# Loads unit by unit in the order of need, full-array kv and inter, and crossbar transposes from unit 10 on, in a linear-attention and bilinear-FFN kernel

## Chip, cores, metric

One core of one Trainium2 chip. The metric is device time in microseconds (us). "Span" is the time from the first to the last instruction in a profiled run; a run's time is about 2 us longer than its span. The diffs are shortened; words in them stand for longer code.

## The reference

Block-recurrent linear attention with a decay per head (4 batches, 8 heads, 768 positions, 64 dims), then a bilinear FFN on its output:

```python
for b in range(nb):                      # blocks of 64 positions
    intra = einsum('bhic,bhjc->bhij', qb, kb) * Dmask      # lam ** (i-j), lower triangle
    out_b = einsum('bhij,bhjd->bhid', intra, vb) + einsum('bhid,bhde->bhie', qb*lam_pow, kv)
    kv = lam**block * kv + einsum('bhsd,bhse->bhde', kb*rev_pow, vb)
x = out.transpose(0, 2, 1, 3).reshape(3072, 512)
y = ((x @ w_a) * (x @ w_b)) @ w_out      # w_a, w_b: 512 x 1536, w_out: 1536 x 512; all float32
```

## The kernel before

The kernel works in units of 128 positions of one batch, with all 8 heads; 24 units, 6 to a batch. It scales q and k by powers of lam, so that the decay needs only a triangle mask and a running state. Four units make a group of 512 tokens. While TensorE does one group's FFN, "hooks" between its matmuls insert the attention of the next group: `prep` (scale q and k, cast v), T (transpose q and k), K (the scores and their mask), O (output, inter from the state, and the state's update kv). Slots 0 to 11 are the hooks after each of the 12 chunks of a and b, slots 12 to 19 lie in the op matmuls, two per token tile. The schedule is written by hand: each engine has its instructions in one fixed order, and all DMAs are issued from one queue, SP's, in a fixed order too.

```python
def load_batch(b, n0=0, n1=NB):
    ...                                   # allocate qf, kf, vf of the whole batch, two buffers each
    for t, src in zip(batch_tiles[b], (qr, kr, vr)):
        if n0 == 0 and n1 == NB:          # whole batch: 1.5 MB per tensor
            nc.sync.dma_start(out=t[:].rearrange("p h nb d -> p (h nb) d"), in_=...)
        else:                             # tensor by tensor, unit by unit
            for nb in range(n0, n1):
                nc.sync.dma_start(out=t[:, :, nb, :], in_=src[b, :, :, nb, :])

def piece_T(u):                           # 8 transposes on TensorE, copied out by ScalarE
    for j, src in enumerate((d["qs"], d["ks"])):
        for hp in range(HP):
            nc.tensor.transpose(tps[:, j, hp, :], src[:, 2 * hp:2 * hp + 2, :], ident)
    nc.scalar.copy(qkT, tps)

def piece_O(u, xT, col):
    ...                                   # 8 matmuls vb x masked scores, then, in half arrays:
    for hp in range(HP):
        for i in range(2):
            p = slice(64 * i, 64 * i + 64)
            nc.tensor.matmul(o_ps[p, hp, :], lhsT=st[p, hp, :], rhs=qkT[p, 0, hp, :], ...)        # inter
    ...
            nc.tensor.matmul(kvd[p, hp, :], lhsT=ks[:, 2 * hp + i, :], rhs=vb[:, 2 * hp + i, :], ...)  # kv
    nc.vector.tensor_copy(st, kvd)

# order of loads: units 0-3, w_a and w_b chunk 0, w_a chunk 1; then
load_w("b", 1); load_w("a", 2); load_batch(0, UPG, NB)          # units 4 and 5
preps = {0: 0, 3: 1, 8: 2, 12: 3}
base, offs = [0, 4, 9, 14], [(1, 2, 4), (1, 2, 4), (1, 2, 3), (1, 2, 3)]   # slots of T, K, O
def hook(slot):
    if g == 0:
        ...
        if slot == 3: ...; load_w("o", 1)
        if slot == 4: ...; load_w("o", 2); load_batch(1)
    if slot in preps:
        u = nxt * UPG + preps[slot]
        prep(u)
        if u % NB == NB - 1 and u // NB + 2 < B:
            load_batch(u // NB + 2)
    ...
```

## Time and profile before

| | before |
|---|---|
| time, median of 3 | 306.51 us (304.59 to 306.56) |
| span, profiled run | 304.6 us, mean granted clock 0.938 |
| TensorE busy | 238.3 us, 78% |
| lead-in (to the first a_ps matmul) | 35.1 us |
| first group's FFN | 79.9 us |
| a later group of four | 38.4 us |

Busy shares mix stages with different limits. What matters is where TensorE waits: the lead-in, and a hole from 58 to 92 us in the first group. The prediction below shows those lines. In SP's timeline (start, duration, queue, source line, DMA), whole-batch loads have line L92.

### The profile page before, as it was taken

What the parts mean: (1) busy time and instruction counts of PE and PEld (TensorE: products, weight loads), DVE (VectorE), ACT (ScalarE), POOL (GpSimd) and SP (SyncE); (2) the same over time, 40 slices, a digit from 0 to 9 for tenths busy, and PEclk for the clock granted to TensorE, in tenths of its full rate; (3) what the DMA queues carried; (4) which work ended last, traced back from release to release, by engine and by line L of the source; (5) the groups of instructions that cost most, each with busy time, mean ns of one, the idle gap of its engine ahead of it and who ended that gap; (6) DMA issues with size and microseconds to landing.
All of it is one profiled execution on the core that took longest, in us unless ns stands there. A gap on an engine that the chain in (4) does not pass through costs nothing.

```text
span 304.6 us, 4308 instructions
## 1 busy us (share of the span) xinstructions
PE 238.3 (78%) x1760; PEld 116.0 (38%) x1760; DVE 102.6 (34%) x168; ACT 103.3 (34%) x156; POOL 53.5 (18%) x56
## 2 busy tenths in 40 slices
PE   0205899600007699999999999999999999999995
PEld 0104544200002254444444444454454444444442
DVE  2113695000002523464125542264512554213410
ACT  4027475200002134533344334434344343333321
POOL 1500332000019621212212121212211000000000
PEclk9999999955557799999999999999999999999999
DMA  7999969999997016930910001100011000110002
GB/s 146 218 337 387 219 221 290 218 218 277 217 218 138 37 69 157 220 75 22 253 72 0 2 0 74 67 3 0 2 69 69 3 0 2 69 71 0 0 34 103
DMA packets 41059, 34.87 MB, mean 114 GB/s; under 512 B 19536, under 2 KB 33360, under 8 KB 41040
## 3 DMA queue, kind: packets, MB, share of 16 engines
q1 hardware_dynamic: 41040, 34.61, 46.1%
q8 instruction: 13, 0.21, 0.3%
q14 instruction: 6, 0.05, 0.1%
HBM read 28.32 MB, written 6.29 MB: 114 GB/s over the span
## 4 chain that ended last, share of the span: by engine, by line
PE 66%; SPq 16%; DMA 8%; DVE 5%; issue 2%; ACT 2%; DVEq 0%; ACTq 0%
PE op L255 19%; PE a_ps L242 18%; PE b_ps L248 17%; SPq L92 9%; DMA vf<-in_v_dram 5%; SPq L96 4%; PE tps L182 3%; DVE m L199 3%; DMA wst<-in_moe_w_b_dram 3%; PE o_ps L210 2%; SPq L109 2%; PE kq L194 2%; PE o_ps L217 2%; PE kvd L227 1%; DVE ab L250 1%
## 5 line engine op out<-in xcount | busy, mean ns | idle before, releaser
L250 DVE TENSOR_TENSOR ab<-a_sb,b_ps 128x512 bf16<-128x512 bf16 x72 | 49.3, 687 | 86.0 <-PE b_ps L248 85.8
L242 PE MATMUL a_ps<-xT,wa_sb 128*128 128x512 bf16 x288 | 75.0, 383 | 0.4 <-ACT xT L219 0.4
L248 PE MATMUL b_ps<-xT,wb_sb 128*128 128x512 bf16 x288 | 74.8, 383 | 0.0
L255 PE MATMUL op<-wo_sb,ab 128*128 128x512 bf16 x288 | 68.3, 387 | 0.0
L245 ACT CAST a_sb<-a_ps 128x512 bf16<-128x512 f32 x72 | 42.2, 587 | 58.3 <-PE a_ps L242 58.3
L199 DVE TENSOR_TENSOR m<-kq,lotri 128x512 bf16<-128x512 f32 x48 | 30.8, 683 | 35.2 <-PE kq L194 35.1
L248 PEld LDWEIGHTS <-wb_sb 128*128 128x128 bf16 x288 | 28.4, 98 | 34.6 <-issue 1.1
L184 ACT COPY qkT<-tps 128x1024 bf16<-128x1024 bf16 x24 | 24.2, 1013 | 45.1 <-PE tps L182 45.1
L169 POOL TENSOR_TENSOR qs<-qf,lp_q 128x512 bf16<-128x512 f32 x20 | 20.8, 1041 | 102.1 <-PE tps L182 49.7
L255 PEld LDWEIGHTS <-ab 128*128 128x128 bf16 x288 | 26.7, 99 | 30.9 <-issue 2.3
L170 POOL TENSOR_TENSOR ks<-kf,lp_k 128x512 bf16<-128x512 f32 x24 | 26.3, 1098 | 65.9 <-PE kvd L227 39.3
L242 PEld LDWEIGHTS <-wa_sb 128*128 128x128 bf16 x288 | 26.1, 98 | 27.9 <-issue 1.0
L182 PE MATMUL tps<-ident,qs 128*128 128x128 bf16 x96 | 10.4, 238 | 32.6 <-POOL qs L169 26.2
L260 ACT COPY o_sb<-op 128x512 f32<-128x512 f32 x24 | 14.0, 585 | 46.8 <-PE op L255 46.8
L174 DVE CAST vb<-vf 128x512 bf16<-128x512 f32 x20 | 10.8, 540 | 42.7 <-DMA vf<-in_v_dram 42.7
L219 ACT CAST xT<-o_ps 128x512 bf16<-128x512 f32 x24 | 14.0, 585 | 30.1 <-PE o_ps L217 18.7
L182 PEld LDWEIGHTS <-qs 128*128 128x128 bf16 x96 | 7.7, 106 | 37.8 <-POOL qs L169 26.7
L194 PE MATMUL kq<-qkT 64*128 64x128 bf16 x192 | 10.3, 231 | 14.0 <-ACT qkT L184 14.0
L182 PE MATMUL tps<-ident,ks 128*128 128x128 bf16 x96 | 10.4, 238 | 10.8 <-POOL ks L170 10.7
L210 PE MATMUL o_ps<-m,vb 128*64 128x128 bf16 x192 | 11.6, 230 | 4.8 <-DVE m L199 4.2
L194 PEld LDWEIGHTS <-qkT 64*128 64x128 bf16 x192 | 5.8, 99 | 23.6 <-ACT qkT L184 16.8
L210 PEld LDWEIGHTS <-vb 128*64 128x64 bf16 x192 | 7.0, 112 | 14.7 <-issue 8.4
(26 smaller groups left out, 65.3 us busy)
## 6 DMA issues: line engine op xcount, KB each, us to landing
out_dram<-o_sb SPq DMA_DIRECT2D x24, 256.0 KB, 2.0
wst<-in_moe_w_a_dram SPq DMA_DIRECT2D x3, 1024.0 KB, 6.5
wst<-in_moe_w_b_dram SPq DMA_DIRECT2D x3, 1024.0 KB, 6.9
wst<-in_moe_w_out_dram SPq DMA_DIRECT2D x3, 1024.0 KB, 7.3
qf<-in_q_dram SPq DMA_DIRECT2D x6, 256.0 KB, 4.9
kf<-in_k_dram SPq DMA_DIRECT2D x6, 256.0 KB, 5.1
vf<-in_v_dram SPq DMA_DIRECT2D x6, 256.0 KB, 5.1
qf<-in_q_dram SPq DMA_DIRECT2D x3, 0.2 KB, 12.5
```

Source lines behind the costliest of these rows:

```text
L92: nc.sync.dma_start(out=t[:].rearrange("p h nb d -> p (h nb) d"), in_=src[b].rearrange("p h nb d -> p (h nb) d"))
L170: nc.gpsimd.tensor_mul(ks, kf[:, :, nb, :], lk)
L182: nc.tensor.transpose(tps[:, j, hp, :], src[:, 2 * hp:2 * hp + 2, :], ident)
L184: nc.scalar.copy(qkT, tps)
L194: nc.tensor.matmul(kq[i][:, hp, :], lhsT=qkT[p, 1, hp, :], rhs=qkT[p, 0, hp, :], start=True, stop=True, skip_group_check=True)
L199: nc.vector.tensor_mul(m, kq[i], lotri_bc)
L210: nc.tensor.matmul(o_ps[p, hp, :], lhsT=vb[:, 2 * hp + i, :], rhs=m[i][:, hp, :], start=(hp == 0), stop=(nb == 0), skip_group_check=True)
L242: nc.tensor.matmul(a_ps, lhsT=wa_sb[:, s, fsl], rhs=xT[:, s, :], start=(s == 0), stop=(s == KS - 1))
L245: nc.scalar.copy(a_sb, a_ps)
L248: nc.tensor.matmul(b_ps, lhsT=wb_sb[:, s, fsl], rhs=xT[:, s, :], start=(s == 0), stop=(s == KS - 1))
L250: nc.vector.tensor_mul(ab[:, f, :], a_sb, b_ps)
L255: nc.tensor.matmul(op, lhsT=ab[:, f, t * 128:(t + 1) * 128], rhs=wo_sb[:, f, :], start=(f == 0), stop=(f == FC - 1))
```

## The change

The intent is threefold. Loads go out unit by unit in the order in which they are needed, with groups of 4, 2, 4, 4, 4, 4, 2 units, so that only two units have to be there early. kv and inter use the full 128x128 array (4 matmuls for 8) at the price of a masked copy of the state. From unit 10 on, the DMA crossbar transposes q and k, in place of TensorE and ScalarE.

```diff
+GROUPS = (4, 2, 4, 4, 4, 4, 2)
+W_CHUNKS = (256, 256, 512, 512)
+LOOKAHEAD = 6
+DMA_T_FROM = 10
+def piece_plan(n_cur, n_next, first):
+    if first:          where = [(15, 16, 17), (17, 18, 19)]
+    elif n_cur == 2:   where = [(1, 3, 5), (6, 8, 10), (10, 11, 12), (13, 14, 15)]
+    elif n_next == 2:  where = [(2, 4, 6), (9, 12, 14)]
+    else:              where = [(1, 2, 4), (5, 6, 8), (10, 11, 13), (15, 16, 17)]
 ...
-wst bufs=3, ld bufs=2 (whole batches)
+wst bufs=6, ld bufs=LOOKAHEAD (single units)
+    def load_unit(u):
+        for n, src in (("qf", qr), ("kf", kr), ("vf", vr)):
+            t = ld_pool.tile([128, H, D], F32, name=n, tag=n)
+            nc.sync.dma_start(out=t, in_=src[b, nb])
 ...
+    # prep: after scaling into qk
+        if u >= DMA_T_FROM:
+            nc.sync.dma_start_transpose(out=qkT[:].rearrange("p j hp i -> p (j hp) i"),
+                                        in_=qk[:].rearrange("p j h d -> p (j h d)"))
 ...
+    # piece_O, inter ahead of the masked scores, and kv
+                nc.tensor.matmul(o_ps[:, hp, :], lhsT=kv["st"][:, hp, :], rhs=qkT[:, 0, hp, :], ...)
+                nc.tensor.matmul(kv["ps"][:, hp, :], lhsT=qk[:, 1, 2 * hp:2 * hp + 2, :],
+                                 rhs=vb[:, 2 * hp:2 * hp + 2, :], ...)
+            nc.vector.tensor_mul(st, kv["ps"], bdiag_bc)
 ...
-    cast_w("a", 0, "dve"); cast_w("b", 0, "act")        # ahead of the lead-in's pieces
+        if step == 2:                                    # inside them
+            cast_w("a", 0, "dve"); cast_w("b", 0, "act"); load_w("a", 3); load_w("b", 3)
 ...
+                if slot == 2: ...; load_w("o", 2); prefetch(n0 + LOOKAHEAD)
+            for kk in prep_at.get(slot, ()):             # two slots ahead of T
+                prep(u); prefetch(u + 1 + LOOKAHEAD)
```

More of the change, by code (lines that the diff above doesn't have):

```diff
@@ L25, in _bc @@
     return dataclasses.replace(ap, ap=dims)
+GROUPS = (4, 2, 4, 4, 4, 4, 2)
[3 more added lines that the diff above has]
+def piece_plan(n_cur, n_next, first):
+    if n_next == 0:
+        return {}
+    if first:
+        where = [(15, 16, 17), (17, 18, 19)]
+    elif n_cur == 2:
+        where = [(1, 3, 5), (6, 8, 10), (10, 11, 12), (13, 14, 15)]
+    elif n_next == 2:
+        where = [(2, 4, 6), (9, 12, 14)]
+    else:
+        where = [(1, 2, 4), (5, 6, 8), (10, 11, 13), (15, 16, 17)]
+    plan = {}
+    for k, w in enumerate(where[:n_next]):
+        for name, s in zip("TKO", w):
+            plan.setdefault(s, []).append((name, k))
+    return plan
 @with_exitstack
@@ L47 @@
     assert D == 64 and d_model == H * D
-    N_TOK = B * S
-    GT = 512
-    NG = N_TOK // GT
-    UPG = GT // BLK
+    NU = B * NB
+    assert sum(GROUPS) == NU
     KS = d_model // 128
     FC = d_ff // 128
-    WCH = 512
-    NWC = d_ff // WCH
     PSUM = bass.MemoryType.PSUM
     singles = ctx.enter_context(tc.tile_pool(name="singles", bufs=1))
-    wst_pool = ctx.enter_context(tc.tile_pool(name="wst", bufs=3))
-    ld_pool = ctx.enter_context(tc.tile_pool(name="ld", bufs=2))
+    wst_pool = ctx.enter_context(tc.tile_pool(name="wst", bufs=6))
+    ld_pool = ctx.enter_context(tc.tile_pool(name="ld", bufs=LOOKAHEAD))
     prep_pool = ctx.enter_context(tc.tile_pool(name="prep", bufs=4))
@@ L63 @@
     msk_pool = ctx.enter_context(tc.tile_pool(name="msk", bufs=2))
-    kv_pool = ctx.enter_context(tc.tile_pool(name="kv", bufs=2))
+    st_pool = ctx.enter_context(tc.tile_pool(name="st", bufs=2))
     xT_pool = ctx.enter_context(tc.tile_pool(name="xT", bufs=2))
@@ L75, in ps_bank @@
         return ps_pool.tile(shape, dt, name=name, tag="ps")
-    qr = q.rearrange("b h (nb p) d -> b p h nb d", p=BLK)
-    kr = k.rearrange("b h (nb p) d -> b p h nb d", p=BLK)
-    vr = v.rearrange("b h (nb p) d -> b p h nb d", p=BLK)
-    batch_tiles = {}
-    def alloc_batch(b):
-        batch_tiles[b] = tuple(
-            ld_pool.tile([128, H, NB, D], F32, name=n, tag=n) for n in ("qf", "kf", "vf"))
-    def load_batch(b, n0=0, n1=NB):
-        if b not in batch_tiles:
-            alloc_batch(b)
-        for t, src in zip(batch_tiles[b], (qr, kr, vr)):
-            if n0 == 0 and n1 == NB:
-                nc.sync.dma_start(out=t[:].rearrange("p h nb d -> p (h nb) d"),
-                                  in_=src[b].rearrange("p h nb d -> p (h nb) d"))
-            else:
-                for nb in range(n0, n1):
-                    nc.sync.dma_start(out=t[:, :, nb, :], in_=src[b, :, :, nb, :])
+    qr = q.rearrange("b h (nb p) d -> b nb p h d", p=BLK)
+    kr = k.rearrange("b h (nb p) d -> b nb p h d", p=BLK)
+    vr = v.rearrange("b h (nb p) d -> b nb p h d", p=BLK)
+    raw = {}
+    def load_unit(u):
+        b, nb = divmod(u, NB)
+        ts = []
+        for n, src in (("qf", qr), ("kf", kr), ("vf", vr)):
+            t = ld_pool.tile([128, H, D], F32, name=n, tag=n)
+            nc.sync.dma_start(out=t, in_=src[b, nb])
+            ts.append(t)
+        raw[u] = ts
     wa_sb = singles.tile([128, KS, d_ff], BF16, name="wa_sb")
@@ L103 @@
     wo_r = moe_w_out.rearrange("(ko p) n -> p ko n", p=128)
+    w_off = [sum(W_CHUNKS[:i]) for i in range(len(W_CHUNKS) + 1)]
     staged = {}
     def load_w(kind, c):
-        t = wst_pool.tile([128, 4, WCH], F32, name="wst", tag="wst")
+        w = W_CHUNKS[c] if kind != "o" else 512
+        t = wst_pool.tile([128, 4, 512], F32, name="wst", tag="wst")
         if kind == "o":
@@ L111, in load_w @@
             r = wa_r if kind == "a" else wb_r
-            nc.sync.dma_start(out=t, in_=r[:, :, c * WCH:(c + 1) * WCH])
+            nc.sync.dma_start(out=t[:, :, :w], in_=r[:, :, w_off[c]:w_off[c] + w])
         staged[kind, c] = t
@@ L117, in cast_w @@
         if kind == "o":
-            dst = wo_sb[:, 4 * c:4 * c + 4, :]
+            dst, src = wo_sb[:, 4 * c:4 * c + 4, :], t
         else:
-            dst = (wa_sb if kind == "a" else wb_sb)[:, :, c * WCH:(c + 1) * WCH]
+            w = W_CHUNKS[c]
+            dst = (wa_sb if kind == "a" else wb_sb)[:, :, w_off[c]:w_off[c] + w]
+            src = t[:, :, :w]
         if eng == "act":
-            nc.scalar.copy(dst, t)
+            nc.scalar.copy(dst, src)
         elif eng == "dve":
-            nc.vector.tensor_copy(dst, t)
+            nc.vector.tensor_copy(dst, src)
         else:
-            nc.gpsimd.tensor_copy(dst, t)
+            nc.gpsimd.tensor_copy(dst, src)
     lam_sb = singles.tile([128, H], F32, name="lam_sb")
@@ L130 @@
                                               ap=[[0, 128], lam.ap[0]]))
-    load_batch(0, 0, UPG)
-    load_w("a", 0)
-    load_w("b", 0)
-    load_w("a", 1)
+    for u in range(GROUPS[0]):
+        load_unit(u)
+    for c in range(3):
+        load_w("a", c)
+        load_w("b", c)
     loglam = singles.tile([128, H], F32, name="loglam")
@@ L147 @@
                             base=0, pattern=[[1, 128]], channel_multiplier=-1)
+    bdiag = singles.tile([128, 2, 64], BF16, name="bdiag")
+    nc.gpsimd.memset(bdiag, 0.0)
+    nc.gpsimd.memset(bdiag[0:64, 0, :], 1.0)
+    nc.gpsimd.memset(bdiag[64:128, 1, :], 1.0)
     tmpe = singles.tile([128, NB, H], F32, name="tmpe")
@@ L155 @@
     lotri_bc = _bc(lotri, [lotri.ap[0], [0, HP], lotri.ap[1]])
+    bdiag_bc = _bc(bdiag, [bdiag.ap[0], [0, HP], [1, 128]])
     U = {}
-    kv_state = {}
+    kv = {}
     def prep(u, first=False):
-        b, nb = divmod(u, NB)
-        qf, kf, vf = batch_tiles[b]
-        qs = prep_pool.tile([128, H, D], BF16, name="qs", tag="qs")
-        ks = prep_pool.tile([128, H, D], BF16, name="ks", tag="ks")
+        nb = u % NB
+        qf, kf, vf = raw.pop(u)
+        qk = prep_pool.tile([128, 2, H, D], BF16, name="qk", tag="qk")
         vb = prep_pool.tile([128, H, D], BF16, name="vb", tag="vb")
@@ L168, in prep @@
         lk = lp_k[:, nb].to_broadcast([128, H, D])
-        (nc.vector if first else nc.gpsimd).tensor_mul(qs, qf[:, :, nb, :], lq)
-        nc.gpsimd.tensor_mul(ks, kf[:, :, nb, :], lk)
+        (nc.vector if first else nc.gpsimd).tensor_mul(qk[:, 0], qf, lq)
+        nc.gpsimd.tensor_mul(qk[:, 1], kf, lk)
         if first:
-            nc.scalar.copy(vb, vf[:, :, nb, :])
+            nc.scalar.copy(vb, vf)
         else:
-            nc.vector.tensor_copy(vb, vf[:, :, nb, :])
-        U[u] = dict(qs=qs, ks=ks, vb=vb)
+            nc.vector.tensor_copy(vb, vf)
+        U[u] = dict(qk=qk, vb=vb)
+        if u >= DMA_T_FROM:
+            qkT = qkT_pool.tile([128, 2, HP, 128], BF16, name="qkT", tag="qkT")
+            nc.sync.dma_start_transpose(out=qkT[:].rearrange("p j hp i -> p (j hp) i"),
+                                        in_=qk[:].rearrange("p j h d -> p (j h d)"))
+            U[u]["qkT"] = qkT
     def piece_T(u):
         d = U[u]
+        if "qkT" in d:
+            return
         tps = ps_bank("tps", [128, 2, HP, 128], BF16)
-        for j, src in enumerate((d["qs"], d["ks"])):
+        for j in range(2):
             for hp in range(HP):
-                nc.tensor.transpose(tps[:, j, hp, :], src[:, 2 * hp:2 * hp + 2, :], ident)
+                nc.tensor.transpose(tps[:, j, hp, :], d["qk"][:, j, 2 * hp:2 * hp + 2, :], ident)
         qkT = qkT_pool.tile([128, 2, HP, 128], BF16, name="qkT", tag="qkT")
@@ L185, in piece_T, with piece_K @@
         d["qkT"] = qkT
-    def piece_KQ(u):
+    def piece_K(u):
         d = U[u]
@@ L202, in piece_O @@
     def piece_O(u, xT, col):
-        b, nb = divmod(u, NB)
+        nb = u % NB
         d = U.pop(u)
-        ks, vb, qkT, m = d["ks"], d["vb"], d["qkT"], d["m"]
+        qk, vb, qkT, m = d["qk"], d["vb"], d["qkT"], d["m"]
         o_ps = ps_bank("o_ps", [128, HP, 128], F32)
+        if nb > 0:
+            for hp in range(HP):
+                nc.tensor.matmul(o_ps[:, hp, :], lhsT=kv["st"][:, hp, :], rhs=qkT[:, 0, hp, :],
+                                 start=(hp == 0), stop=False, skip_group_check=True)
         for hp in range(HP):
@@ L210, in piece_O @@
                 nc.tensor.matmul(o_ps[p, hp, :], lhsT=vb[:, 2 * hp + i, :], rhs=m[i][:, hp, :],
-                                 start=(hp == 0), stop=(nb == 0), skip_group_check=True)
-        if nb > 0:
-            st = kv_state[b]
-            for hp in range(HP):
-                for i in range(2):
-                    p = slice(64 * i, 64 * i + 64)
-                    nc.tensor.matmul(o_ps[p, hp, :], lhsT=st[p, hp, :], rhs=qkT[p, 0, hp, :],
-                                     start=False, stop=True, skip_group_check=True)
+                                 start=(nb == 0 and hp == 0), stop=True, skip_group_check=True)
         nc.scalar.copy(xT[:, :, col:col + BLK], o_ps)
@@ L221, in piece_O @@
             if nb == 0:
-                kv_state["ps"] = kvps_pool.tile([128, HP, D], F32, name="kvd", tag="kvd")
-            kvd = kv_state["ps"]
+                kv["ps"] = kvps_pool.tile([128, HP, 128], F32, name="kvd", tag="kvd")
             for hp in range(HP):
-                for i in range(2):
-                    p = slice(64 * i, 64 * i + 64)
-                    nc.tensor.matmul(kvd[p, hp, :], lhsT=ks[:, 2 * hp + i, :], rhs=vb[:, 2 * hp + i, :],
-                                     start=(nb == 0 and hp == 0), stop=True, skip_group_check=True)
@@ L229, in piece_O @@
-            st = kv_pool.tile([128, HP, D], BF16, name="st", tag="st")
-            nc.vector.tensor_copy(st, kvd)
-            kv_state[b] = st
+                nc.tensor.matmul(kv["ps"][:, hp, :], lhsT=qk[:, 1, 2 * hp:2 * hp + 2, :],
+                                 rhs=vb[:, 2 * hp:2 * hp + 2, :],
+                                 start=(nb == 0 and hp == 0), stop=True, skip_group_check=True)
+            st = st_pool.tile([128, HP, 128], BF16, name="st", tag="st")
+            nc.vector.tensor_mul(st, kv["ps"], bdiag_bc)
@@ L234, with ffn @@
+            kv["st"] = st
     out_r = out.rearrange("(t p) n -> t p n", p=128)
-    def ffn(g, xT, hook):
-        ab = ab_pool.tile([128, FC, GT], BF16, name="ab", tag="ab")
+    def ffn(u0, n, xT, hook):
+        gt = n * BLK
+        ab = ab_pool.tile([128, FC, 512], BF16, name="ab", tag="ab")
         for f in range(FC):
             fsl = slice(f * 128, (f + 1) * 128)
-            a_ps = ps_bank("a_ps", [128, GT], F32)
+            a_ps = ps_bank("a_ps", [128, 512], F32)
             for s in range(KS):
-                nc.tensor.matmul(a_ps, lhsT=wa_sb[:, s, fsl], rhs=xT[:, s, :],
+                nc.tensor.matmul(a_ps[:, :gt], lhsT=wa_sb[:, s, fsl], rhs=xT[:, s, :gt],
@@ L243, in ffn @@
                                  start=(s == 0), stop=(s == KS - 1))
-            a_sb = a_pool.tile([128, GT], BF16, name="a_sb", tag="a")
-            nc.scalar.copy(a_sb, a_ps)
-            b_ps = ps_bank("b_ps", [128, GT], F32)
+            a_sb = a_pool.tile([128, 512], BF16, name="a_sb", tag="a")
+            nc.scalar.copy(a_sb[:, :gt], a_ps[:, :gt])
+            b_ps = ps_bank("b_ps", [128, 512], F32)
             for s in range(KS):
-                nc.tensor.matmul(b_ps, lhsT=wb_sb[:, s, fsl], rhs=xT[:, s, :],
+                nc.tensor.matmul(b_ps[:, :gt], lhsT=wb_sb[:, s, fsl], rhs=xT[:, s, :gt],
@@ L249, in ffn @@
                                  start=(s == 0), stop=(s == KS - 1))
-            nc.vector.tensor_mul(ab[:, f, :], a_sb, b_ps)
+            nc.vector.tensor_mul(ab[:, f, :gt], a_sb[:, :gt], b_ps[:, :gt])
             hook(f)
-        for t in range(UPG):
+        for t in range(n):
             op = ps_bank("op", [128, d_model], F32)
@@ L260, in ffn @@
             nc.scalar.copy(o_sb, op)
-            nc.sync.dma_start(out=out_r[g * UPG + t], in_=o_sb)
+            nc.sync.dma_start(out=out_r[u0 + t], in_=o_sb)
             hook(FC + 2 * t + 1)
@@ L267, in new_xT, with prefetch, hook @@
     def new_xT(g):
-        xTs[g] = xT_pool.tile([128, KS, GT], BF16, name="xT", tag="xT")
+        xTs[g] = xT_pool.tile([128, KS, 512], BF16, name="xT", tag="xT")
+    g_u0 = [sum(GROUPS[:i]) for i in range(len(GROUPS))]
     new_xT(0)
-    for u in range(UPG):
+    n0 = GROUPS[0]
+    for u in range(n0):
         prep(u, first=True)
-    cast_w("a", 0, "dve")
-    cast_w("b", 0, "act")
-    load_w("b", 1)
-    load_w("a", 2)
-    load_batch(0, UPG, NB)
-    for step in range(UPG + 2):
-        if step < UPG:
+    for step in range(n0 + 2):
+        if step < n0:
             piece_T(step)
-        if 0 <= step - 1 < UPG:
-            piece_KQ(step - 1)
-        if 0 <= step - 2 < UPG:
+        if 0 <= step - 1 < n0:
+            piece_K(step - 1)
+        if 0 <= step - 2 < n0:
             piece_O(step - 2, xTs[0], (step - 2) * BLK)
-    plan = {}
-    base = [0, 4, 9, 14]
-    offs = [(1, 2, 4), (1, 2, 4), (1, 2, 3), (1, 2, 3)]
-    for kk in range(UPG):
-        for name, o in zip("TKO", offs[kk]):
-            plan.setdefault(base[kk] + o, []).append((name, kk))
-    preps = {0: 0, 3: 1, 8: 2, 12: 3}
-    for g in range(NG):
-        nxt = g + 1
-        if nxt < NG:
-            new_xT(nxt)
-        def hook(slot, g=g, nxt=nxt):
+        if step == 2:
+            cast_w("a", 0, "dve")
+            cast_w("b", 0, "act")
+            load_w("a", 3)
+            load_w("b", 3)
+    next_load = [n0]
+    def prefetch(limit):
+        while next_load[0] < min(NU, limit):
+            load_unit(next_load[0])
+            next_load[0] += 1
+    for g, n in enumerate(GROUPS):
+        n_next = GROUPS[g + 1] if g + 1 < len(GROUPS) else 0
+        if n_next:
+            new_xT(g + 1)
+        plan = piece_plan(n, n_next, g == 0)
+        prep_at = {}
+        for s, ps in plan.items():
+            for name, kk in ps:
+                if name == "T":
+                    prep_at.setdefault(max(0, s - 2), []).append(kk)
+        def hook(slot, g=g, n_next=n_next, plan=plan, prep_at=prep_at):
             if g == 0:
@@ L303, in hook @@
                     cast_w("a", 1, "dve")
-                    load_w("b", 2)
-                if slot == 1:
                     cast_w("b", 1, "act")
                     load_w("o", 0)
-                if slot == 3:
+                    load_w("o", 1)
+                if slot == 2:
                     cast_w("a", 2, "dve")
-                    load_w("o", 1)
-                if slot == 4:
                     cast_w("b", 2, "act")
                     load_w("o", 2)
-                    load_batch(1)
-                if slot == 7:
-                    cast_w("o", 0, "pool")
-                if slot == 9:
-                    cast_w("o", 1, "pool")
-                if slot == 10:
-                    cast_w("o", 2, "pool")
-            if nxt >= NG:
-                return
-            if slot in preps:
-                u = nxt * UPG + preps[slot]
+                    prefetch(n0 + LOOKAHEAD)
+                if slot == 6:
+                    cast_w("a", 3, "dve")
+                    cast_w("b", 3, "act")
+                if slot in (9, 10, 11):
+                    cast_w("o", slot - 9, "pool")
+            for kk in prep_at.get(slot, ()):
+                u = g_u0[g + 1] + kk
                 prep(u)
-                if u % NB == NB - 1 and u // NB + 2 < B:
-                    load_batch(u // NB + 2)
+                prefetch(u + 1 + LOOKAHEAD)
             for name, kk in plan.get(slot, ()):
-                u = nxt * UPG + kk
+                u = g_u0[g + 1] + kk
                 if name == "T":
@@ L332, in hook @@
                 elif name == "K":
-                    piece_KQ(u)
+                    piece_K(u)
                 else:
-                    piece_O(u, xTs[nxt], kk * BLK)
-        ffn(g, xTs[g], hook)
-        del xTs[g]
+                    piece_O(u, xTs[g + 1], kk * BLK)
+        ffn(g_u0[g], n, xTs.pop(g), hook)
 _INS = ['q', 'k', 'v', 'lam', 'moe_w_a', 'moe_w_b', 'moe_w_out']
```

## The prediction

> **What bounds the kernel now.** I read the page's slices first, then the chain of waits in order of time, then the timeline around the hole that they show, and last the groups of instructions for durations.
>
> The slices (40 of 7.6 us each):
>
> ```profile
> PE   0205899600007699999999999999999999999995
> PEclk9999999955557799999999999999999999999999
> DMA  7999969999997016930910001100011000110002
> GB/s 146 218 337 387 219 221 290 218 218 277 217 218 138 37 69 157 220 75 22 253 72 0 2 0 74 67 3 0 2 69 69 3 0 2 69 71 0 0 34 103
> ```
>
> Three stretches. TensorE does little in the first four slices. It works, then stops from about 58 to 92 us, with the granted clock down to 0.5, while the DMA row is full. From 115 us to the end it is full and the DMA row nearly empty. So the first third is bound by loads and the rest by TensorE. The timeline through the hole says which loads:
>
> ```profile
> 47.25 8.94 SPq L92 DMA_DIRECT2D kf<-in_k_dram  x1
> 56.64 6.74 SPq L92 DMA_DIRECT2D vf<-in_v_dram  x1
> 63.49 7.06 SPq L109 DMA_DIRECT2D wst<-in_moe_w_out_dram  x1
> ...
> 83.39 1.04 POOL L169 TENSOR_TENSOR qs<-qf,lp_q 128x512 bf16<-128x512 f32 x1 [33.85 <-DMA qf<-in_q_dram]
> 84.48 0.61 PE L182 MATMUL tps<-ident,qs 128*128 128x128 bf16 x4 [26.24 <-POOL qs L169]
> 90.62 1.04 POOL L170 TENSOR_TENSOR ks<-kf,lp_k 128x512 bf16<-128x512 f32 x1 [6.20 <-DMA kf<-in_k_dram]
> 97.47 1.15 DVE L174 CAST vb<-vf 128x512 bf16<-128x512 f32 x1 [42.68 <-DMA vf<-in_v_dram]
> ```
>
> The second FFN group needs units 6 and 7, the first of batch 1. They come only with whole-batch loads of 1.5 MB (6.7 to 8.9 us of queue time each), and TensorE, in program order, stops at the transposes of unit 6. The first group's FFN runs from 35.08 us (first a_ps) to 114.96 us (the next group's first a_ps): 79.9 us. An undisturbed group takes 38.4 (192.50 to 230.92 in the chain).
>
> The lead-in, same view:
>
> ```profile
> 18.07 0.62 ACT L172 CAST vb<-vf 128x512 bf16<-128x512 f32 x1 [0.46 <-DMA vf<-in_v_dram]
> 23.49 1.90 ACT L122 CAST wb_sb<-wst 128x2048 bf16<-128x2048 f32 x1 [4.80 <-DMA wst<-in_moe_w_b_dram]
> 25.29 1.92 ACT L184 COPY qkT<-tps 128x1024 bf16<-128x1024 bf16 x2
> 35.08 1.02 PE L242 MATMUL a_ps<-xT,wa_sb 128*128 128x512 bf16 x4 [0.43 <-ACT xT L219]
> ```
>
> ScalarE has the last v cast at 18.7, then stands behind a weight cast whose load lands at 23.5, so the first qkT copy starts at 25.3 although its transposes are long done.
>
> The groups that the change touches on TensorE:
>
> ```profile
> L182 PE MATMUL tps<-ident,qs 128*128 128x128 bf16 x96 | 10.4, 238 | 32.6 <-POOL qs L169 26.2
> L182 PE MATMUL tps<-ident,ks 128*128 128x128 bf16 x96 | 10.4, 238 | 10.8 <-POOL ks L170 10.7
> L217 PE MATMUL o_ps<-qkT,st 64*64 64x128 bf16 x160 | 8.2, 222 | 0.0
> L227 PE MATMUL kvd<-vb,ks 128*64 128x64 bf16 x160 | 6.4, 203 | 0.0
> ```
>
> Matmuls overlap, so these durations are no costs; I take start-to-start distances from the timeline of the 192 to 231 us group: the 8 transposes of a unit 0.45 us (195.79 to 196.24), K 0.43 with its gap, the 8 O matmuls 0.34, inter 0.34, kv 0.24 and 0.1 of gap. A unit costs 1.9 us, the FFN of four units 31.1 (20.7 a and b, 10.4 op, from the last group, which has no attention beside it).
>
> **What the skill says.** (1) "TensorE: Matmul & The Clock Gate", section "Wait — 56ns, not 53.3ns?", gives 55.6 ns between warm matmuls of 128 columns; the trace agrees (0.45 us / 8 = 56 ns), and I use it for the 4+4 full-array matmuls. (2) "Perfetto Trace Analysis", section "What 'DMA-bound' means", lists a DMA sequencer solid with slices; the trace agrees: from 47 to 88 us the SP queue is nearly unbroken issue. (3) "VectorE: DVE Perf Modes", section "The three transpose paths", gives 1309 ns for a 128x128 bf16 transpose by the crossbar. (4) "DMA: Bandwidth & Descriptors", section "Latency and other measured facts", gives 261 GB/s for one kernel's DMA transposes. No run here shows (3) or (4), and they disagree: a unit is 128x1024 bf16, 256 KB, so by (4) 1.0 us plus landing, by (3) as eight in series 10.5 us.
>
> **The change part by part** (us of span).
>
> *Lead-in.* Twelve loads of 256 KB at 1.14 us each, as now: the last v is again cast by 18.7. The b cast now follows step 2, so qkT starts at 18.7 instead of 25.3: -6.6. The a cast in VectorE's stream (0.7 for half of a 1.47 us cast) and wider st multiplies (0.68 like the mask multiply, for 0.42) give back 1.0. FFN starts at 29.5.
>
> *Do loads keep up?* After unit 3: 1 MB of weights twice, then 2 MB, 2 MB and 3 MB of w_out, at about 280 to 380 GB/s (slices 3 and 4: 337 and 387), done near 45 us. Units 4 to 9 are queued behind it at some 3.6 us each (3 x 1.14 plus gaps): unit 4 lands near 48.5, 5 near 52, 9 near 66. Unit 4's v is first touched at slot 13, 29.5 + 20.7 + 2.6 + 1.5 = 54; unit 6 after 67. Each has 5 us or more to spare, and later ones are six ahead. So the 41 us excess of the first group goes entirely, as does the slow clock.
>
> *Group lengths.* Attention per unit becomes T 0.45, K 0.43, O 0.34 + inter 4 x 0.056 = 0.22 + kv 0.22 + gap 0.1 = 0.9: 1.8 with T, 1.35 without. Full arrays save about 0.13 a unit, 2.6 in 20 units; the missing T saves 14 x 0.45 = 6.3 (the 1.01 us qkT copies on ScalarE were beside other work).
> - Group 0: 31.1 + 2 x 1.8 + 2.5 of stalls (weight casts; T, K, O of units 4 and 5 only one half-op, 1.3 us, apart) = 37.2.
> - Group 1, two units' FFN with four units' attention: 15.6 + 7.2 + 3 of the same stalls = 25.8.
> - Groups 2, 3, 4: 31.1 + 5.4 + 0.3 = 36.8 each, 110.4.
> - Group 5, two next: 31.1 + 2.8 = 33.9. Group 6: 15.6. Tail from the last op to the end as now, 304.6 - 300.9 = 3.7.
>
> Sum 29.5 + 37.2 + 25.8 + 110.4 + 33.9 + 15.6 + 3.7 = 256.1 of span; the profiled run's time is 2.0 over its span (306.61 against 304.6), so 258.1.
>
> *The crossbar.* The transpose sits in the SP queue between stores and loads. SP may run ahead of TensorE (four qk buffers, three qkT buffers), but in each group of four the first transpose stands behind the previous group's last store, and its K is at slot 2: 5.2 - 0.9 = 4.3 us. The fourth stands behind this group's first store, at slot 13, its K at slot 16: three half-ops, 3.9 us. A transpose of L us from issue to landing thus costs about (L-4.3)+(L-3.9) per group, three times: nothing at 3 us, 5.4 at 5, 20 at 8, plus SP's own occupancy. That the split is at unit 10 and not earlier suggests a cost that hurts in the short group 1 (6 us a unit) but not later (9 us), so I take 4.5: +3. Prediction 261.
>
> **Rivals.** (a) The crossbar is slow, 10.5 us a unit. With 3.4 of loads, SP needs 14 us a unit in groups 2 and 3 against 9 of TensorE work: about +20 in each, +15 in group 4, some 316 in all, slower than now. For: figure (3). Against: figure (4). The profile before has no such transfer. (b) Small loads are worse than whole batches: 256 B rows at 217 GB/s (slices 2 and 5) are 87 us for 18.9 MB, and stores queue behind. For: SP took 1.14 us for each. Against: the last use is at 230 us, and now too the full-batch loads run at 217 to 220. If unit 4 came 10 us late, 268. (c) The order by need works, but short groups cost more: ScalarE and VectorE in group 1 (about 12 and 15 of 26 us by these durations) delay T, K, O: +5, 266. (d) The crossbar is free and stalls of mine don't come: 252.
>
> **Range and chances.** The 41 + 5.6 us of removed load waiting are secure; what spreads is the crossbar, mainly upwards. 8 in 10: 250 to 275. Faster by over 2% (below 300.4) fails only if L is near 10: 0.96; within 2% 0.02; slower 0.02.
>
> **What would show it.** Right: first a_ps near 29.5, no zero slices in the PE row after 30 us, the DMA row less full and longer, groups of about 37 us, a qf landing before POOL wants it. For the crossbar: K's wait on qkT, released by a DMA, under 2 us at the first and fourth unit of a group. Wrong: PE waiting for vb or qs in group 0 or 1 (rival b), SP solid with transposes (a), or a lower clock without idling.

## More of the kernel before

```profile
45.98 0.82 SPq L92 DMA_DIRECT2D qf<-in_q_dram  x1
...
70.77 0.70 SPq L92 DMA_DIRECT2D qf<-in_q_dram  x1
...
116.16 0.71 SPq L92 DMA_DIRECT2D qf<-in_q_dram  x1
```

Three batches are loaded, starting at 46, 71 and 116 us.

## The result and the profile after

252.94 us (median of 4, 252.66 to 253.41) against 306.53 for the kernel before: ratio 0.8252, interval 0.8206 to 0.8297. All outputs are right. The prediction said 261 with a range of 250 to 275: the direction and the range held, the point was 8 us too high.

The slices of the page after (40 of 6.3 us):

```profile
PE   0308699999899999999999999999999999999994
PEclk9999999999999999999999999999999999999999
DMA  6999999989999999913979813870005230012102
```

The hole is gone, no slice between the lead-in and the last one falls below 8, and the granted clock never drops. DMA work is longer than before, the crossbar's included (queue q1 takes 68.5% of 251.1 us, 172 us, for 46.1% of 304.6, 140 us, by the two pages), but it lies beside TensorE's. The stages, from the table of busy time by window (columns: window, its length, then busy us and count of PE, PEld, DVE, ACT and POOL, then granted clock, DMA share and GB/s; the windows run from one group's first a_ps to the next's, as the chain of waits dates them, up to 0.16 us later than the timeline):

```profile
29.49:65.90 36.41, 34.82 (x205) 16.38 (x205) 15.73 (x23) 16.78 (x23) 17.41 (x15) 1.00 1.08 274
65.90:89.53 23.63, 22.99 (x244) 16.70 (x244) 13.29 (x28) 11.62 (x22) 6.98 (x8) 1.00 1.10 230
89.53:125.66 36.13, 36.13 (x233) 17.05 (x233) 16.93 (x28) 11.01 (x19) 9.96 (x10) 1.00 0.86 156
125.66:162.01 36.35, 36.26 (x238) 17.26 (x236) 16.46 (x27) 11.68 (x20) 8.17 (x8) 1.00 0.77 145
162.01:198.30 36.29, 36.26 (x238) 17.16 (x236) 17.07 (x28) 11.68 (x20) 4.09 (x4) 1.00 0.25 59
198.30:231.80 33.50, 33.50 (x190) 15.59 (x189) 12.10 (x19) 10.53 (x18) 0.00 (x0) 1.00 0.17 47
```

The second column against the prediction: 36.4 (37.2 said), 23.6 (25.8), 36.1, 36.4, 36.3 (36.8 each), 33.5 (33.9); the lead-in ends at 29.49 (29.5). TensorE is busy all but 1.6 us of the first of these windows and all but 0.1 of the third to sixth. The first group, 79.9 us before, takes 36.4: 43.5 us, the bulk of the 53.5 us of span. (Some 3.6 us of that are only moved: the first group now prepares two units for the next one instead of four, at 1.8 us each by the prediction's terms.)

The groups that answer to those of before (by source line: transposes L213, inter L240):

```profile
L213 PE MATMUL tps<-ident,qk 128*128 128x128 bf16 x80 | 7.8, 247 | 9.1 <-DVE qk L193 7.6
...
L240 PE MATMUL o_ps<-qkT,st 128*128 128x128 bf16 x80 | 7.8, 219 | 1.7 <-DVE st L256 1.7
```

Transposes are 80 for 192 (10 units for 24), inter 80 for 160. The mean of one hardly moves, 219 for 222 ns: with pipelined matmuls the busy column tells no gain. Start-to-start times do, and for inter they show almost none (0.31 us for 0.34, see e2).

The lead-in, in the timeline after:

```profile
18.14 0.62 ACT L196 CAST vb<-vf 128x512 bf16<-128x512 f32 x1 [2.89 <-DMA vf<-in_v_dram]
18.66 1.92 ACT L215 COPY qkT<-tps 128x1024 bf16<-128x1024 bf16 x2
```

ScalarE goes from the last v cast straight to the first qkT copy, 6.6 us sooner than before. And the crossbar, from the view of tile qkT (a DMA's issue: min/median/max of its time in the queue in ns; who waited; time to landing):

```profile
L202 SPq DMA_TRANSPOSE qkT<-qk x14: 1255/1296/2309, 89.4 to 200.8; - x14
...
  DMA qkT<-qk: 1.5, 3
...
DMA to landing us min/median/max: 3.1/3.5/6.2
```

A transpose of 128x1024 bf16 holds SP for 1.3 to 2.3 us and lands 3.5 us after its issue at the median. The 1.5 us are waits of K's weight loads alone; by the view of waits no matmul of K stood for a crossbar transpose.

### The profile page after: what moved, and what is told of

Its sections match the earlier page's. It is cut to its first block, busy times and chain, and to the rows that moved or that the text cites. A ratio compares the mean times of both kernels' runs of the same rounds, so it can differ in the third digit from the quotient of the medians. Undisturbed runs are those within 1.5% of the kernel's fastest.

```text
span 251.1 us, 4077 instructions
## 1 busy us (share of the span) xinstructions
PE 225.7 (90%) x1584; PEld 118.4 (47%) x1584; DVE 107.3 (43%) x181; ACT 92.0 (37%) x155; POOL 52.4 (21%) x59
## 3 DMA queue, kind: packets, MB, share of 16 engines
q1 hardware_dynamic: 99072, 38.29, 68.5%
## 4 chain that ended last, share of the span: by engine, by line
PE 80%; SPq 5%; issue 4%; DVE 4%; DMA 3%; ACT 2%; DVEq 0%; POOL 0%
PE a_ps L269 24%; PE b_ps L275 23%; PE op L282 22%; SPq L109 5%; PE kq L225 3%; PE o_ps L245 2%; DMA vf<-in_v_dram 2%; PE kvd L252 2%; DVE m L230 2%; DMA qkT<-qk 1%; PE tps L213 1%; PE o_ps L240 1%; DVE wa_sb L143 1%; ACT xT L247 1%; ACT o_sb L287 1%
## 5 line engine op out<-in xcount | busy, mean ns | idle before, releaser
L277 DVE TENSOR_TENSOR ab<-a_sb,b_ps 128x512 bf16<-128x512 bf16 (+1 forms) x84 | 51.2, 611 | 84.6 <-PE b_ps L275 71.1
L269 PE MATMUL a_ps<-xT,wa_sb 128*128 128x512 bf16 (+1 forms) x336 | 76.1, 349 | 2.3 <-ACT xT L247 1.4
L275 PE MATMUL b_ps<-xT,wb_sb 128*128 128x512 bf16 (+1 forms) x336 | 76.0, 349 | 0.0
L272 ACT CAST a_sb<-a_ps 128x512 bf16<-128x512 f32 (+1 forms) x84 | 44.1, 525 | 71.6 <-PE a_ps L269 71.5
L193 POOL TENSOR_TENSOR qk<-qf,lp_q 128x512 bf16<-128x512 f32 x20 | 20.8, 1042 | 94.9 <-PE kvd L252 49.6
L194 POOL TENSOR_TENSOR qk<-kf,lp_k 128x512 bf16<-128x512 f32 x24 | 25.0, 1042 | 11.4 <-DMA kf<-in_k_dram 11.3
L256 DVE TENSOR_TENSOR st<-kvd,bdiag 128x512 bf16<-128x512 f32 x20 | 13.8, 689 | 11.7 <-PE kvd L252 11.3
L213 PE MATMUL tps<-ident,qk 128*128 128x128 bf16 x80 | 7.8, 247 | 9.1 <-DVE qk L193 7.6
L213 PEld LDWEIGHTS <-qk 128*128 128x128 bf16 x80 | 5.9, 111 | 10.6 <-DVE qk L193 7.8
L215 ACT COPY qkT<-tps 128x1024 bf16<-128x1024 bf16 x10 | 10.0, 1013 | 2.1 <-PE tps L213 2.1
L240 PE MATMUL o_ps<-qkT,st 128*128 128x128 bf16 x80 | 7.8, 219 | 1.7 <-DVE st L256 1.7
```

The source lines that it names most:

```text
L193: (nc.vector if first else nc.gpsimd).tensor_mul(qk[:, 0], qf, lq)
L194: nc.gpsimd.tensor_mul(qk[:, 1], kf, lk)
L213: nc.tensor.transpose(tps[:, j, hp, :], d["qk"][:, j, 2 * hp:2 * hp + 2, :], ident)
L269: nc.tensor.matmul(a_ps[:, :gt], lhsT=wa_sb[:, s, fsl], rhs=xT[:, s, :gt], start=(s == 0), stop=(s == KS - 1))
L272: nc.scalar.copy(a_sb[:, :gt], a_ps[:, :gt])
L275: nc.tensor.matmul(b_ps[:, :gt], lhsT=wb_sb[:, s, fsl], rhs=xT[:, s, :gt], start=(s == 0), stop=(s == KS - 1))
```

## The experiments

The prediction was right in number, so the questions were which part gives what, and whether its reasons hold. On the view of the profile, one thing did not fit the prediction's reason for the hole ("they come only with whole-batch loads"): the code calls for batch 2 at slot 3, in the hook that prepares unit 5, and for batch 1 at slot 4. The batch loaded from 46 us on, two of whose lines the prediction shows, is then batch 2, which nobody needs before unit 12, and batch 1 is the one issued at 71, whose q reached GpSimd at 83.39. So there were two theories for the 41 us: **grain** (mine) and **order**.

Results, with the kernel before on the same chip in each case:

| run | median us | runs | before | ratio | interval |
|---|---|---|---|---|---|
| f1_batch_order | 285.44 | 4 | 307.35 | 0.9279 | 0.9235-0.9324 |
| f2_batch1_by_unit | 267.51 | 4 | 307.35 | 0.8705 | 0.8665-0.8745 |
| e1_no_xbar | 259.16 | 4 | 307.35 | 0.8427 | 0.8394-0.8461 |
| e2_half_arrays | 254.66 | 4 | 307.35 | 0.8285 | 0.8251-0.8319 |
| after_again | 253.07 | 4 | 307.27 | 0.8236 | 0.8218-0.8255 |
| e3_groups_of_4 | 269.95 | 4 | 307.27 | 0.8791 | 0.8767-0.8816 |
| e5_xbar_twice | 257.93 | 4 | 307.27 | 0.8393 | 0.8374-0.8413 |
| g1_lead_in | 251.72 | 6 | 307.27 | 0.8202 | 0.8173-0.8230 |
| e4_xbar_from_6 | 262.74 | 4 | 306.69 | 0.8544 | 0.8505-0.8584 |
| e6_groups_of_4_w_first | 258.93 | 4 | 306.69 | 0.8432 | 0.8399-0.8466 |
| g2_warm | 254.64 | 6 | 306.69 | 0.8282 | 0.8247-0.8318 |
| g3_warm_xbar_11 | 249.02 | 6 | 307.26 | 0.8117 | 0.8081-0.8153 |

Not all runs were on the same chip; the kernel before differs by 0.3% between them. Differences below are of medians; worked out from the ratios they come out within 0.3 us of these.

### f1: the kernel before, batches in order

```diff
-                if u % NB == NB - 1 and u // NB + 2 < B:
-                    load_batch(u // NB + 2)
+                if u % NB == 1 and u >= NB and u // NB + 1 < B:
+                    load_batch(u // NB + 1)
```

> The kernel before with one thing changed: the whole-batch loads are issued as batch 1, 2, 3. In the kernel before, batch 2 is called for at slot 3 of the first group and batch 1 only at slot 4, so 4.7 MB that nobody needs yet stand ahead of units 6 and 7. Theory of order: batch 1 takes the place of batch 2 in the queue, its last v lands near 75 us instead of 97, so TensorE resumes some 25 us sooner: 281 us. Theory of grain (what the prediction named, whole batches of 1.5 MB): nothing changes, 306 us. If order is all, the whole 41 us go: 266.

Measured 285.44, 21.9 us below the kernel before, where the theory of order said 281. Its timeline:

```profile
46.92 0.83 SPq L92 DMA_DIRECT2D qf<-in_q_dram  x1
...
61.58 1.04 POOL L169 TENSOR_TENSOR qs<-qf,lp_q 128x512 bf16<-128x512 f32 x1 [12.77 <-DMA qf<-in_q_dram]
...
68.84 1.04 POOL L170 TENSOR_TENSOR ks<-kf,lp_k 128x512 bf16<-128x512 f32 x1 [6.22 <-DMA kf<-in_k_dram]
...
75.91 0.94 DVE L174 CAST vb<-vf 128x512 bf16<-128x512 f32 x1 [21.53 <-DMA vf<-in_v_dram]
```

Batch 1's q, k and v reach the engines at 61.6, 68.8 and 75.9 us, where the kernel before had 83.4, 90.6 and 97.5: each 21.6 to 21.8 us sooner, which is what the batch that stood ahead takes (4.7 MB at 217 GB/s: 21.7). Order is confirmed, and grain alone is refuted as the whole cause. But the hole has not gone: unit 6 still waits for three whole tensors.

### f2: and batch 1 by units

```diff
 # as f1, and at slot 4
-                    load_batch(1)
+                    for n in range(NB):
+                        load_batch(1, n, n + 1)
```

> As f1, and batch 1 is loaded unit by unit. Unit 6 should land near 59 us, about where TensorE asks for it: the hole shrinks to 3 to 5 us and the time to about 269 us. If the grain gives nothing once the order is right, it stays with f1.

Measured 267.51: another 17.9 us. In its chain of waits the first a_ps of the first and of the second group:

```profile
36.00 1.02 PE a_ps L242 x4
...
76.12 0.86 PE a_ps L242 x4
```

The first group now lasts 40.1 us for 79.9. So order and grain share the hole, 22 and 18 us, and these two edits alone, with everything else of the kernel before, give 40 of the 54 us. The split holds for this sequence of edits: batch 1 in units with batch 2 still ahead of it was not run.

### e1: no crossbar

```diff
-DMA_T_FROM = 10
+DMA_T_FROM = 24
```

> The changed kernel with all transposes on TensorE (threshold 24). The prediction's step: 14 x 0.45 us come back on TensorE, 259 us. Rival: the K piece would have waited anyway, or the crossbar's own waits eat the gain: 253 us. Third: the crossbar's loads and stalls cost more than it saves: below 252.

Measured 259.16, 6.1 us above the changed kernel's 253.07. The step of 14 x 0.45 = 6.3 us holds to 0.2 us. The traces place the loss where the transposes are: the first a_ps of group 2 comes at 89.45 us (89.53 in the changed kernel), and from there to that of group 6 it is 148.1 us for 142.1. The missing transposes are on the path, and the crossbar gives back almost nothing.

### e2: half arrays again

```diff
-   4 inter matmuls lhsT=kv["st"][:, hp, :], 4 kv matmuls, tensor_mul(st, kv["ps"], bdiag_bc)
+   8 inter matmuls lhsT=kv["st"][p, hp, :], 8 kv matmuls, tensor_copy(st, kv["ps"])
```

> The changed kernel with kv and inter in half arrays again (8 matmuls each in place of 4, state copied, not masked). The prediction's step: 0.13 us in 20 units, 2.6 us: 255.5 us. Rival: the wider mask multiply on VectorE (0.69 for 0.42 us) had eaten it: 253 us or less.

Measured 254.66, 1.6 us above 253.07 (the intervals of the ratios just touch, but no run of one falls among the other's). The sign is right, the reason is not. TensorE's pieces inter, O and kv of one unit, in the changed kernel and then in e2:

```profile
142.81 0.39 PE L240 MATMUL o_ps<-qkT,st 128*128 128x128 bf16 x4
143.12 0.41 PE L245 MATMUL o_ps<-m,vb 128*64 128x128 bf16 x8
143.47 0.40 PE L252 MATMUL kvd<-vb,qk 128*128 128x128 bf16 x4
...
143.02 0.41 PE L242 MATMUL o_ps<-qkT,st 64*64 64x128 bf16 x8
143.37 0.41 PE L247 MATMUL o_ps<-m,vb 128*64 128x128 bf16 x8
143.61 0.29 PE L256 MATMUL kvd<-vb,qk 128*64 128x64 bf16 x8
```

The next piece starts at 143.71 and 143.84. From start to start the three take 0.90 us with full arrays and 0.82 with half arrays, and the other units between 100 and 240 us agree (inter 0.31 and 0.34, O 0.35 and 0.24, kv 0.24 and 0.23): on TensorE half arrays cost nothing here. (Why O is shorter with them is open.) What e2 loses lies at two K pieces, at 157.95 and 195.27 us, whose matmuls waited 0.93 and 1.23 us for the crossbar, where the changed kernel's never did. Why those transposes landed later is open (the first held SP for 2.62 us, 1.76 in the changed kernel). So a gain of the full arrays themselves is not shown.

### e3 and e6: groups of four

```diff
-GROUPS = (4, 2, 4, 4, 4, 4, 2)
+GROUPS = (4, 4, 4, 4, 4, 4)          # with the general plan also for the first group
 # e3: prefetch(n0 + LOOKAHEAD) ahead of the first FFN, instead of after load_w("o", 2)
 # e6: prefetch(n0 + 2) there, the rest after load_w("o", 2)
```

> The changed kernel with six groups of four; so that units 4 to 9 exist when the first group asks for them at slot 0, their loads go ahead of the w_out loads. If the short second group is what lets the loads keep up: w_out lands near 60 us where TensorE wants it near 56, 6 to 8 us of waiting, 260 us. If the order alone does it: 253 us or, without the stalls of the short group, 251.

Measured 269.95, more than either theory said. It was a poor experiment: the prefetch of later units in the first preps put unit 10 too ahead of the last w_out chunk, and TensorE waited for w_out until 73 us. It shows again what order costs, not what grouping does. Next, e6 loads in the order that such groups need.

> The changed kernel with six groups of four again, but loads in the order in which such groups need them: units 4 and 5, then w_out, then units 6 on. If the short second group matters even in the right order (unit 6's v, wanted near 47 us, lands near 54): 257 to 259 us. If order was all: 251 to 253.

Measured 258.93, as expected in number, 5.9 us above the changed kernel. The reason is another than I wrote: not unit 6's v but unit 4's q is late. In e6's chain of waits (start, duration, what):

```profile
24.94 12.41 DMA qf<-in_q_dram
...
39.62 0.61 PE tps L213 x4
```

With the general plan, unit 4 is wanted at slot 1, about 33 us, and its load is issued at 24.9, behind up to 4 MB of weights still under way. TensorE stands from 33.2 us until the transposes of q at 38.6 and of k at 39.6, and then runs at half pace until about 44 (four matmuls of 512 columns in 1.71 us, 0.86 elsewhere). So the short second group is worth 5.9 us beyond the order of loads: it puts off the first need of a new unit to slot 15. (The load order differs a little too, so this is the price of groups of four with the best order that I tried, not of the group size by itself.)

### e5: each transpose twice

```diff
+            nc.sync.dma_start_transpose(out=dum[:]..., in_=qk[:]...)      # into a tile nobody reads
             nc.sync.dma_start_transpose(out=qkT[:]..., in_=qk[:]...)
```

> The changed kernel with every crossbar transpose issued twice, first into a tile that nobody reads, so that its time to landing grows from 3.5 us (the trace after) by the 1.3 to 2.3 us that one holds the queue. If the slack is what the prediction said (4.3 us at the first unit of a group, 3.9 at the fourth): (5.3 - 4.3) + (5.3 - 3.9) in three groups, some +7: 260 us. If SP runs so far ahead that there is slack to spare: 253 us.

Measured 257.93, 4.9 us above 253.07, where 7 were expected if the slack was as worked out and 0 if SP ran far ahead. The wait of K, from the same view of qkT as above:

```profile
  DMA qkT<-qk: 12.9, 11
```

This view adds up the idle time of weight loads and of matmuls. By the view of waits the matmuls of K alone stood 5.0 us, in five places, where the changed kernel's stood nowhere, and that is the 4.9 us. The five are the fourth unit's K of each of the three groups and the first unit's of two (at 122, 133, 160, 171 and 198 us): the places where the prediction had put the slack. So there is little of it: one more transpose in the queue, 1.3 to 2.3 us, already shows at TensorE. The crossbar is nearly free here because 3.5 us just fit, not because there is room.

### e4: crossbar from unit 6

```diff
-DMA_T_FROM = 10
+DMA_T_FROM = 6
```

> The changed kernel with the crossbar from unit 6 on. The prediction took the threshold of 10 as a sign that it costs too much in the short group. By the trace after, SP is issuing loads without a break until 87 us and stores are 8 us late, so the transpose of unit 6 could not be issued before 73 us, while its K stands at 70: 4 x 0.45 saved, some 6 lost, 257 us. If only the 3.5 us to landing count: 251 us.

Measured 262.74, slower by 9.7 us than the changed kernel. The timeline: SP's last store ahead of the transpose, the transpose, and unit 6's K with the wait before it:

```profile
71.51 1.39 SPq L288 DMA_DIRECT2D out_dram<-o_sb  x2
73.01 1.62 SPq L202 DMA_TRANSPOSE qkT<-qk  x1
...
78.17 0.61 PE L225 MATMUL kq<-qkT 64*128 64x128 bf16 x8 [8.28 <-DMA qkT<-qk]
```

The transpose was issued at 73.0 us, as worked out, but its K came 5.2 us later, so TensorE stood for 8.3 us instead of 6, and ran the next chunks at half pace (groups of four matmuls of 256 columns follow each other at 0.85 us, at 0.44 before the wait). The trace puts it down to the queue: GpSimd had scaled unit 6's q and k by 55.6 us, but SP was working off loads and stores without a break, and the transpose had to stand in line. No run puts the transposes on another queue to test that.

### g1, g2, g3: what is left in the lead-in

The experiments pointed at ScalarE's order in the lead-in, where qkT of unit 0 could be copied at 8 us but stands behind the last v cast at 18.1.

```diff
 # g1
-    for u in range(n0): prep(u, first=True)
     for step in range(n0 + 2):
         if step < n0:
+            prep(step, first=True)
             piece_T(step)
-        if step == 2: cast_w("a", 0, "dve") ...
+        if step == 4: cast_w("a", 0, "dve") ...
 # g2: g1 and matmuls on a tile of zeros, 8 before the loop and 6 after each of steps 0 to 2
+            nc.tensor.matmul(w_ps, lhsT=ident, rhs=warm, start=True, stop=True)
 # g3: g2 and
-DMA_T_FROM = 10
+DMA_T_FROM = 11
```

> The changed kernel with the preparation of each of the first four units written just before its transposes, and the first two weight casts at the end of the lead-in, so that ScalarE no longer holds the first qkT copy (ready at 8 us) behind the last v cast (18.1 us). Unit 3's chain from its v: FFN starts near 23 us in place of 29.5, but then runs into the weight loads (a third chunk near 31, w_out near 45): net -4, 249 us. If the weights bind at once: 252. If nothing on ScalarE was in the way: 253.

Measured 251.72 (250.6 to 253.2), only 1.4 us better, with overlapping intervals: not settled as a gain. Its FFN starts at 27.17, not 23, because TensorE runs at half pace through the whole lead-in (4 kv matmuls 0.55 us, 0.24 later on), and the chain of pieces from unit 3's v on is as much TensorE's as VectorE's. The next run tests the half pace.

> g1 with matmuls on zeros in TensorE's waits of the lead-in (8 of 512 columns at the start, 6 after each of the first three steps), so that it does not run at half pace there: in g1 and after, 8 transposes take 0.97 us until 23 to 28 us and 0.45 later. If that half pace is what ate g1's gain: FFN starts near 25 in place of 27.2, 249 us. If the chain is bound by loads or by VectorE: 251.5 us.

Measured 254.64: a miss. The FFN did start at 24.95, as expected, 2.2 us sooner than in g1, and group 2 started at 84.62 instead of 89.53. But there it met the queue:

```profile
89.73 1.39 SPq L202 DMA_TRANSPOSE qkT<-qk  x1
...
94.16 0.61 PE L225 MATMUL kq<-qkT 64*128 64x128 bf16 x8 [4.21 <-DMA qkT<-qk]
94.70 1.89 PE L269 MATMUL a_ps<-xT,wa_sb 128*128 128x512 bf16 x4
```

SP works off its loads until 87 us in either kernel, so the transpose of unit 10 goes out at 89.7 where it went at 89.4 before; only TensorE now wants it 5 us sooner. It waits 4.2 us, and then takes 6.1 us for 16 matmuls that take 3.5 elsewhere: together nearly 7 us lost, more than the 5 won.

> g2 with the crossbar from unit 11 instead of 10. In g2 the FFN did start at 25 us and group 2 at 84.6, but SP was still issuing loads until 88, so the crossbar transpose of unit 10 landed at 94, TensorE waited 7 us for it and ran slowly after that. If that queue is the whole of g2's loss: the lead-in's 4.5 us come through, less 0.45 for unit 10's transposes on TensorE: 248.4 us. If the stall only moves on to unit 11: 252 to 254 us.

Measured 249.02. With unit 10 on TensorE, its K runs without a wait:

```profile
90.24 0.40 PE L225 MATMUL kq<-qkT 64*128 64x128 bf16 x8
```

So the queue was g2's loss. Against the changed kernel this is 0.8117 / 0.8236 = 0.986, with intervals apart: the best version, 1.4% faster. Its six runs fall on two levels, three near 248.0 (the 248.4 expected) and three near 250.2. The slower three show a granted clock of 0.993, the others 0.997 to 1.0; why is open.

## Why the prediction was right, point by point

1. **Lead-in, 29.5 us.** Right: 29.49. Both terms are in the timeline: the first qkT copy comes 6.6 us sooner, and from it to the first a_ps it is 10.8 us for 9.8. No run takes the lead-in's edits out one by one.
2. **The hole goes entirely.** Right in its effect (36.4 us for 79.9). Its cause was half read. I took the whole-batch loads as the reason; f1 and f2 show 22 us from the order of the batches and 18 from their size. The effect did not hang on that: it was worked out from when the units land in the new order. The code had it, in two neighbouring slots, and I did not ask whose data the queue was moving in the hole.
3. **Loads keep up with 5 us or more to spare.** Right for the loads: no v cast waits for one after the lead-in. (One sign of being right failed: GpSimd did wait for a q in three places, 4.3 us in all. It cost nothing, as TensorE did not want these units yet.) I had not asked what stands behind them in the same queue. SP is busy with loads until 87 us, stores are issued 8 us late (62.8 us for a tile done at 54.8), and a transpose has to stand behind all that. e4 and g2 both fell over it.
4. **Missing T, 6.3 us.** Right: 6.1 (e1).
5. **Full arrays, 2.6 us.** Not shown, and the reason was wrong. I counted inter as four matmuls at 0.056, 0.22 us for 0.34; from its start to the next piece it takes 0.31. The sum of 0.9 for O, inter and kv came out all the same (0.35 + 0.31 + 0.24), because the 0.1 of gap that I had added is not there: by luck. The 1.6 us of e2 come with waits for the crossbar.
6. **Crossbar, +3 us.** Too large: L is 3.5 us at the median where I took 4.5, and no matmul of K waited. The slack of about 4 us was right in kind: e5 made it visible, at the units named. The pessimistic rival (10.5 us a unit) is dead. Two sums in it were wrong, without effect on the point: at 8 us the formula gives 23.4, not 20, and 258.1 with 20, 20 and 15 makes 313, not 316.
7. **The threshold at unit 10 as a sign of cost in the short group.** The conclusion was right, e4 loses 9.7 us below it, but the reason was not the cost per unit against 6 us of TensorE work. It is where the transpose stands in SP's queue.
8. **Stalls in group 1, 3 us.** Too large: the window is 23.6 us for 25.8, 2.2 of the 8 us that the point was off; the crossbar's 3 and 0.4 to 0.8 in each of the other groups make the rest.

The parts as measured: order 21.9, grain 17.9, crossbar 6.1, the lead-in about 5.6 (35.1 to 29.5, read from the traces only). That is 51.5 for a difference of 53.6 to 54.2; where the other 2 to 3 us come from is open. The parts were taken out of different kernels, so that the sum nearly fits is support, not proof, that little is left. The short second group is no further term on top of them: f2 has none and gets by with groups of four, because there units 4 and 5 are loaded before the later weights.

## What to carry to other kernels

When an engine waits for loads, ask first whose data the queue moves during the wait: putting the same transfers in the order of need gave 21.9 us here, before cutting them into small ones gave 17.9, and it was an edit of two lines. A DMA with a consumer close behind it, like a crossbar transpose, is as late as the queue that it stands in; time its place in the queue, not only its own duration. Take the cost of a piece from start-to-start times and not from the count of its matmuls: four for eight saved TensorE next to nothing here. And a stage made faster meets the next limit at an earlier time: g2 lost its 4.5 us to a queue that had just fitted, and got most of them back by moving one unit off it.

## What the Trainium skill lacked or had wrong

- **Cost of a crossbar transpose from SBUF to SBUF.** "VectorE: DVE Perf Modes" (The three transpose paths) has 1309 ns for 128x128 and "DMA: Bandwidth & Descriptors" (Latency and other measured facts) a bandwidth, 261 GB/s. What one does to the issuing queue they do not say in time: a table in the latter's part on trn3 counts sequencer cycles of transposes for "previous generations", without the size of a tile. In the profile after, 128x1024 bf16 held the queue for 1.3 to 2.3 us and landed after 3.1 to 6.2 (median 3.5). Of the prediction's two estimates from these figures, 10.5 us for eight in series is three times that median, and 1.0 us leaves the landing out.
- **Rows of 256 B.** "DMA: Bandwidth & Descriptors" (Why small descriptors are slow) puts the bus overhead at 27% for 256 B, and names the descriptor's own bytes as a second cost, without a sum. The slice of the changed kernel with only such rows ran at 217 GB/s, the two with nearly only weight rows of 2 KB at 386: 44% less. In the unbroken run of loads from 44 to 62 us, 13 of 15 loads of 256 KB in such rows held SP for 0.98 to 1.24 us each, a figure that no page has.
- **Half pace that the granted clock does not show.** "TensorE: Matmul & The Clock Gate" has the cold and the warm pace (Wait — 56ns, not 53.3ns?) and warns that the throttle events in a trace are not fully to be trusted (Seeing it yourself); it has no case like this one. In the lead-in of the changed kernel the granted clock reads 1.00 from the start, while 8 transposes take 0.97 us (20.26 to 21.22), and 0.45 later. Start-to-start times in the timeline show it. After the waits of 4 and 8 us in g2 and e4 the next chunks also ran at half pace, and there the row does show it (0.55 and 0.50).
